# Grouped-query attention on one core: V in 8 KB rows, 64x64 PV tiles, K of two pairs' tiles with alternating heads, a loop of six steps

## The chip, the core and the metric

The kernel runs on one core of one Trainium2 chip. A core has a matrix engine (TensorE, "PE" in the profile, its weight loads "PEld"), a vector engine (VectorE, "DVE"), a scalar engine (ScalarE, "ACT"), a general engine (GpSimd, "POOL") and a sync engine (SyncE, "SP") that here only issues transfers. 16 DMA engines move data between HBM and SBUF, the on-chip memory of 128 partitions; PE writes its results to PSUM, eight banks of 512 fp32 values per partition. The metric is the time of one execution in microseconds (us), the median of several runs.

## What is computed

```python
B, Hq, Hkv, Sq, Sk, D = 16, 32, 8, 16, 2048, 128
...
k = jnp.repeat(k, rep, axis=1)
v = jnp.repeat(v, rep, axis=1)
scale = D ** -0.5
scores = jnp.einsum("bhqd,bhkd->bhqk", q, k) * scale
p = _softmax(scores, axis=-1)
return jnp.einsum("bhqk,bhkd->bhqd", p, v)
```

All tensors are bf16. Four query heads share one K/V head (`rep` is 4), so each K/V head meets 4 x 16 = 64 query rows. There are 128 K/V heads, each with 512 KB of K and 512 KB of V: 134 MB that are read once, and 4 MB of queries and outputs.

## The kernel before

**Work is done by pairs.** A pair is two neighbouring K/V heads: `NP` is 64 pairs, and the 64 query rows of both heads fill the 128 partitions. K of a pair is one transfer of 1 MB (L186), 128 rows of 8 KB: partition `a` holds 32 consecutive keys of one head, head 0 in partitions 0 to 63, head 1 in the rest. V of a pair is one transfer of 1 MB (L194) of 256 rows of 4 KB: each partition takes 16 consecutive keys of both heads. The last pair's V comes in two halves (L199). Q comes in 16 transfers of 128 KB, four pairs each, in rows of 1 KB (L207). The output of a pair is stored in rows of 256 B (L212). All these transfers are issued by SP, in one written order: in turn `t`, K of pair `t`, a Q chunk where one is due, V of pair `t - 5`, the store of pair `t - 12`. A K transfer waits until the transposed use of its buffer six pairs before is done (`sem_kt`), a V transfer until PV of eight pairs before is done (`sem_pv`), a store until the scaling of its pair is done (`sem_nm`).

**K is transposed on DVE** (L342) in 32x32 blocks, as fp32 words that each hold two bf16 values, in two instructions of 1024 words per partition. So 32 partitions of the result hold 32 pairs of head dimensions for a quarter of the keys. **Q** is copied four times side by side by POOL (L175), transposed by PE with an identity (L251) and copied out of PSUM by ACT (L380), so each group of 32 partitions has its own copy.

**Scores** (L273 and L232) take 32 matmuls of 32 rows x 64 columns and 512 moving values per pair: row group `r` goes with column group `r // 2`, so four of the array's eight 32x64 tiles are in use. Half of them (L232) reuse weights that the matmul before loaded. All four PSUM banks of `S_ps` are used, once: the next pair's scores wait until DVE has read them (`sem_max`).

**Softmax.** DVE multiplies the scores by `-scale`, writes them to `Sneg` and accumulates the minimum (L360), ACT takes the exponential and the row sum (L390) and writes bf16 values in an order in which two keys form one fp32 word. PE transposes those words (L284), eight 128x128 transposes per pair in two staging banks of `ST_ps` (a third is Q's), and ACT copies them to `PT` (L400). **PV** (L301) takes 32 matmuls of 128 rows x 64 columns and 128 moving values, one for each head and each of 16 key groups. ACT scales the result by the reciprocal of the row sum (L410; the reciprocal is DVE's, L351).

**Order on PE.** In step `p`: scores of `p + 1`, PV of `p - 3`, transposes of `p`, and in two steps of four a part of the next Q. Eight steps form the body of a hardware loop; the first steps and the last are written out. ACT's order is exponential, scaling, copies; DVE's is minimum, reciprocal, transposes of the pair after next.

## Time and profile before

| | |
|---|---|
| median of 3 runs | 343.18 us (343.05 to 344.3) |
| the profiled execution's own time | 344.2 us |
| its span, first to last instruction | 342.4 us |
| mean granted clock of PE | 0.994 |
| HBM read / written | 136.31 MB / 2.10 MB |
| K: issue to landing, median | 15.9 us |
| V: issue to landing, median | 16.5 us |
| exponential (L390), mean of one | 2494 ns |
| minimum (L360), mean of one | 2256 ns |
| K transposed, half a pair (L342), mean of one | 1222 ns |

In the profile's page, the first part gives each engine's busy time, its share of the span and its number of instructions. The second cuts the span into 40 equal slices: a digit is the busy share in tenths, 9 for 90% or more. The line on packets counts the single DMA descriptors by size. A line of a timeline has the start, the duration, the engine, the source line, the operation and its operands; in brackets stands idle time of the engine just before, and what ended it. A line of the waits has who waited for whom, the sum in us, how often, and the longest. A line of the sums by stretch has its bounds, its length, each engine's busy time and number of instructions, the granted clock, the DMA share and GB/s.

### The profile page before, as it was taken

To read this page: it belongs to the slowest core of one execution; us is meant where nothing else is said; L and a number is where in the kernel's file an instruction comes from. 1 tells how busy PE (TensorE), PEld (TensorE's weight loads), DVE (VectorE), ACT (ScalarE), POOL (GpSimd) and SP (SyncE) were. 2 spreads that over 40 slices of the span, in tenths; PEclk is the share of its full clock that TensorE was granted. 3 is DMA by queue.
4 is the path that set the end of the run, shared out by engine and by line. 5 is a ranking of instruction groups with operands and counts; after the bars stand their busy time and mean duration, and the time that the engine had idled before them with its cause. 6 is when DMAs were issued, how large, how long until landed. Compare 5 with 4: busy or idle time off the path is not lost.

```text
span 342.4 us, 9887 instructions
## 1 busy us (share of the span) xinstructions
PE 279.9 (82%) x4736; PEld 162.4 (47%) x3712; DVE 295.1 (86%) x320; ACT 267.2 (78%) x353; POOL 31.8 (9%) x23
## 2 busy tenths in 40 slices
PE   0677999999999978879788788878879778798785
PEld 0133555555455644535544544535536445455454
DVE  2489999999999998898898888988988979988940
ACT  1178889999888978878788697796887778787792
POOL 3202020202010010202002020020200102000000
PEclk9999999999999999999999999999999999999997
DMA  7999999999999999999999999999999999999993
GB/s 296 421 409 415 415 408 413 416 413 418 413 415 421 413 418 416 412 419 418 412 421 412 417 417 416 418 417 417 414 419 415 418 414 416 420 419 416 414 409 107
DMA packets 38433, 138.63 MB, mean 405 GB/s; under 512 B 11536, under 2 KB 13584, under 8 KB 30224
## 3 DMA queue, kind: packets, MB, share of 16 engines
q1 hardware_dynamic: 38416, 138.43, 100.0%
q8 instruction: 8, 0.13, 0.2%
q14 instruction: 9, 0.07, 0.1%
HBM read 136.31 MB, written 2.10 MB: 404 GB/s over the span
## 4 chain that ended last, share of the span: by engine, by line
DMA 53%; DVE 20%; issue 9%; SPq 8%; PE 8%; ACT 2%; POOL 1%
DMA Vb<-in_v_dram 47%; DVE KT L342 13%; DVE Sneg L360 6%; SPq L186 6%; DMA Kn<-in_k_dram 5%; PE O_ps L301 3%; SPq L212 2%; PE S_ps L273 1%; DMA Qn<-in_q_dram 1%; PE S_ps L232 1%; ACT O L410 1%; PE S_ps L301 1%; PE ST_ps L251 1%; PE ST_ps L284 1%; POOL Q L175 1%
## 5 line engine op out<-in xcount | busy, mean ns | idle before, releaser
L342 DVE STREAM_TRANSPOSE KT<-Kn 128x1024 f32<-128x1024 f32 x128 | 151.4, 1222 | 27.8 <-DMA Kn<-in_k_dram 27.8
L390 ACT ACTIVATE P<-Sneg,nbias 128x2048 bf16<-128x2048 f32 x64 | 159.6, 2494 | 6.3 <-DVE Sneg L360 6.3
L360 DVE TENSOR_SCALAR_CACHE_REDUCE Sneg<-S_ps 128x2048 f32<-128x2048 f32 x64 | 144.4, 2256 | 7.9 <-PE S_ps L232 7.9
L273 PE MATMUL S_ps<-KT,QT 32*64 32x512 bf16 x1024 | 106.0, 395 | 8.0 <-DVE Sneg L360 6.2
L232 PE MATMUL S_ps<-KT,QT 32*64 32x512 bf16 x1024 | 105.0, 388 | 0.0
L301 PE MATMUL O_ps<-Vb,PT 128*64 128x128 bf16 x1952 | 66.2, 221 | 36.6 <-DMA Vb<-in_v_dram 36.6
L301 PEld LDWEIGHTS O_ps<-Vb,PT 128*64 128x64 bf16 x1952 | 56.5, 110 | 78.8 <-issue 43.9
L400 ACT ACTIVATE PT<-ST_ps 128x512 f32<-128x512 f32 x128 | 69.6, 595 | 20.3 <-PE ST_ps L284 20.3
L284 PE MATMUL ST_ps<-ident,P 128*128 128x128 f32 x512 | 70.8, 282 | 4.1 <-ACT P L390 3.3
L273 PEld LDWEIGHTS S_ps<-KT,QT 32*64 32x64 bf16 x1024 | 32.5, 105 | 72.8 <-issue 62.1
L284 PEld LDWEIGHTS ST_ps<-ident,P 128*128 128x128 f32 x512 | 55.5, 142 | 13.4 <-ACT P L390 9.2
L175 POOL COPY Q<-Qn 128x2048 bf16<-128x2048 bf16 x16 | 30.3, 1896 | 255.6 <-PE ST_ps L251 251.8
L410 ACT ACTIVATE O<-O_ps,rrec 128x128 bf16<-128x128 f32 x61 | 22.5, 369 | 34.1 <-PE O_ps L301 33.9
L251 PE MATMUL ST_ps<-ident,Q 128*128 128x128 f32 x128 | 20.2, 282 | 8.8 <-POOL Q L175 8.1
L380 ACT ACTIVATE QT<-ST_ps 128x512 f32<-128x512 f32 x32 | 19.3, 603 | 8.4 <-PE ST_ps L251 8.4
L251 PEld LDWEIGHTS ST_ps<-ident,Q 128*128 128x128 f32 x128 | 15.5, 145 | 9.1 <-issue 8.0
L390 ACT ACTIVATION_READ_ACCUMULATOR P<-Sneg,nbias 128x1 f32 x64 | 13.2, 207 | 0.0
L351 DVE RECIPROCAL rrec<-rowsum 128x1 f32<-128x1 f32 x64 | 10.2, 159 | 3.0 <-ACT P L390 3.0
L301 PE MATMUL S_ps<-Vb,PT 128*64 128x128 bf16 x96 | 3.9, 243 | 2.7 <-DMA Vb<-in_v_dram 1.6
L360 DVE DVE_READ_ACCUMULATOR Sneg<-S_ps 128x1 f32 x64 | 5.4, 84 | 0.0
L301 PEld LDWEIGHTS S_ps<-Vb,PT 128*64 128x64 bf16 x96 | 3.4, 125 | 3.4 <-issue 2.3
L410 ACT ACTIVATE O<-S_ps,rrec 128x128 bf16<-128x128 f32 x3 | 1.1, 370 | 3.4 <-PE S_ps L301 3.4
(8 smaller groups left out, 3.0 us busy)
## 6 DMA issues: line engine op xcount, KB each, us to landing
Kn<-in_k_dram SPq DMA_DIRECT2D x64, 1024.0 KB, 15.9
Vb<-in_v_dram SPq DMA_DIRECT2D x63, 1024.0 KB, 16.5
Qn<-in_q_dram SPq DMA_DIRECT2D x16, 128.0 KB, 15.3
out_dram<-O SPq DMA_DIRECT2D x64, 32.0 KB, 15.4
Vb<-in_v_dram SPq DMA_DIRECT2D x2, 512.0 KB, 12.4
```

The lines of the kernel that those rows point to most:

```text
L175: gp.tensor_copy(Q4[:, :, :, :, :].rearrange("p j b r x -> p (j b) r x"), src.unsqueeze(2).to_broadcast([128, 2 * QPAIRS, 4, 64]),).then_i ...
L186: sp.dma_start(Kn[s][:, :], kf[p]).then_inc(sem_k[s], 16)
L232: return pe.add_instruction(mybir.InstMatmult(name=nc.get_next_instruction_name(), engine=mybir.EngineType.PE, ins=[pe.lower_ap(rhs), pe.l ...
L251: ins = pe.transpose(dst[:, 128 * j:128 * (j + 1)], src[:, j, b, :], ident4[:, :])
L273: ins = pe.matmul(s_ap, w, x, start=(acc == 0), stop=(acc == 3))
L284: ins = pe.transpose(dst[:, 128 * t:128 * (t + 1)], P[p % 2][:, 128 * x:128 * (x + 1)], ident4[:, :])
L301: ins = pe.matmul(o_ap(p)[64 * g:64 * (g + 1), :], pt[:, j // 2, j % 2, 64 * g:64 * (g + 1)], Vb[p % NV][:, g, j, :], start=(j == 0), stop ...
L342: ins = dve.transpose(KT[p % NKT][:, :].rearrange("p (t b e a x) -> p x e t b a", t=J // 2, b=2, e=2, x=2)[:, x, :, :, :, :], Kn[p % NK][: ...
L360: dve.tensor_scalar(Sneg[p % 2][:, :].rearrange("p (t h x) -> p h t x", t=8, h=2), S_ps[:, :].rearrange("p (h t x) -> p h t x", t=8, h=2), ...
L390: act.activation(P[p % 2][:, :].bitcast(BF16).rearrange("p (n y e) -> p n y e", n=16, e=2), Sneg[p % 2][:, :].rearrange("p (n e y) -> p n ...
L400: act.activation(PT[p % NPT][:, 4 * h:4 * (h + 1), :].rearrange("p t q -> p (t q)"), stage_ap(("P", p, h)), ACT.Copy,).then_inc(sem_ev, 1)
L410: act.activation(Osb[p % NO][:, :], o_ap(p), ACT.Copy, scale=rrec[:, p:p + 1]).then_inc(sem_nm, 1)
```

## The change

Work is still done in tiles of two K/V heads, now called units (`NU` is 64), but two units form a double pair `d` (`ND` is 32) of four neighbouring heads 0 to 3.

- *K and scores.* Unit `i` of a double pair holds heads `i` and `i + 2`. Its K is one transfer of 128 rows of 8 KB whose rows alternate between the two heads (partition `2a + g`). The transfer is made by its low-level constructor, as the source has the form 64 x 2 x 4096 and the destination 128 x 1 x 4096. DVE transposes it in one instruction of 2048 words. Each group of 32 partitions now holds a quarter of the keys of both heads, so scores run on all eight 32x64 tiles, each matmul with its own weight load; successive keys of one head lie 8 bytes apart in a moving row, 4 before.
- *V and PV.* V of two neighbouring heads is one transfer of 128 rows of 8 KB: partition `64i + a` has 32 consecutive keys of one head. A PV matmul therefore covers 64 partitions and 64 columns: 128 matmuls of a 64x64 tile for a double pair, in two halves, and the four outputs lie in two PSUM banks. V's buffers are three double pairs (six units, eight before), K's are seven (six before). V of the last double pair goes to K buffers, and its last unit is split 24 to 8 of 32 key groups.
- *Exponential and transposes.* The exponentials of a double pair's two units interleave in one `P` tile, 64 words of each in turn; 16 transposes for a double pair go through two staging banks, the second of them shared with Q (three banks before). On even steps PE waits for ACT's copy of Q (`QW`) ahead of the second group of transposes.
- *Q, stores, order.* Q comes in 32 chunks of two units, 64 KB in rows of 512 B. A store covers 64 partitions x 2 heads, still rows of 256 B. PV runs four steps behind the exponential (three before), stores 13 turns behind K (12 before). PE's loop has six steps and ten rounds, and steps that the last round lacks stand in conditional blocks. The last double pair's scaling is split between ACT and DVE.

The core of the diff:

```diff
-NK = 6
-NV = 8
...
+NK = 7
+NV = 3
+NO = 6
+NQ = 4
+NQT = 3
+NP = 3
+QPAIRS = 2
+BODY = 6
+FIRST = 6
 VLAG = 5
-PVLAG = 3
-SLAG = 12
-QLEAD = 7
+PVLAG = 4
+SLAG = 13
+LASTJ = 24
...
-    kf = k.rearrange("b h s d -> (b h s d)").rearrange("(n a x) -> n a x", n=NP, a=128)
-    vf = v.rearrange("b h s d -> (b h) (s d)").rearrange("g (a x) -> a g x", a=128)
+    kf = k.rearrange("b h s d -> (b h s d)").rearrange("(n g i a x) -> n i a g x", n=ND, g=2, i=2, a=64)
+    vf = v.rearrange("b h s d -> (b h s d)").rearrange("(n a x) -> n a x", n=NU, a=128)
...
+    for u in range(steps):
+        step_at[u] = len(pe_prog)
+        pe_prog.append(("S", u + 1))
+        if u < NU:
+            act_prog.append(("exp", u))
+        d, half = divmod(u - PVLAG, 2)
+        if u >= PVLAG:
+            pe_prog.append(("PV", d, half))
+            if half and d < ND - 1:
+                act_prog += [("norm", d, i) for i in range(2)]
+        if u % 2 == 0:
+            q_part(u, u // 2 + 2)
+        if u >= 1:
+            d, k = divmod(2 * (u - 1), 4)
+            turn(d, k)
+            if u % 2 == 0:
+                pe_prog.append(("QW", u // 2 + 2))
+            turn(d, k + 1)
...
+                sp.add_instruction(mybir.InstDMACopy(
+                    name=nc.get_next_instruction_name(), engine=mybir.EngineType.SP,
+                    ins=sp.lower_ap_dma(kf[m // 2, m % 2]), outs=sp.lower_ap_dma(Kd[s][:, :].unsqueeze(1)),
+                    queue="qSPDynamicHW", mode="Copy", cce_op=ALU.bypass,
+                )).then_inc(sem_k[s], 16)
...
+                d, g = divmod(p, 2)
+                s = d % NV
+                if d == ND - 1:
+                    sp.wait_ge(sem_kt, NU - NK + 2 + g)
+                elif d >= NV and g == 0:
+                    sp.wait_ge(sem_pv, 2 * (d - NV) + 2)
+                for x, (lo, hi) in enumerate([(0, J)] if p < NU - 1 else [(0, LASTJ), (LASTJ, J)]):
+                    dst = v_ap(d, g)[:, lo:hi, :].rearrange("a j d -> a (j d)")
+                    ins = sp.dma_start(dst, vf[p][:, D * lo:D * hi])
+                    ins.then_inc(sem_v[s] if d < ND - 1 else sem_vl[g + x], 16)
...
+                    for acc in range(4):
+                        b, e = divmod(acc, 2)
+                        for z in range(8):
+                            r, g = z % 4, (z + z // 4) % 2
+                            rows = slice(32 * r, 32 * (r + 1))
+                            at = 128 * g + 64 * i
+                            ins = pe.matmul(
+                                S_ps[64 * g:64 * (g + 1), 512 * r:512 * (r + 1)],
+                                qt[rows, b, e, at:at + 64], kt[rows, b, e, g],
+                                start=(acc == 0), stop=(acc == 3),
+                            )
...
+                for j in js:
+                    for g in gs:
+                        for i in range(2):
+                            rows = slice(64 * i, 64 * (i + 1))
                             ins = pe.matmul(
-                                o_ap(p)[64 * g:64 * (g + 1), :],
-                                pt[:, j // 2, j % 2, 64 * g:64 * (g + 1)],
-                                Vb[p % NV][:, g, j, :],
+                                o_ap(d, i)[64 * g:64 * (g + 1), :],
+                                pt[rows, j // 2, j % 2, 64 * g:64 * (g + 1)],
+                                v_ap(d, g)[rows, j, :],
...
+                dve.transpose(
+                    KT[u % 2][:, :].rearrange("p (b j a) -> p j b a", b=2, j=J),
+                    Kd[u % NK][:, :].bitcast(F32).rearrange("p (j b c) -> p j b c", b=2, c=32),
+                ).then_inc(sem_kt, 1)
...
                 dve.tensor_scalar(
-                    Sneg[p % 2][:, :].rearrange("p (t h x) -> p h t x", t=8, h=2),
-                    S_ps[:, :].rearrange("p (h t x) -> p h t x", t=8, h=2), -scale, None,
-                    op0=ALU.mult, op1=ALU.min, accum_out=nbias[:, p:p + 1],
+                    Sneg[u % 2][:, :].rearrange("p (j r a) -> p r j a", j=J, r=4),
+                    S_ps[:, :].rearrange("p (r j a) -> p r j a", j=J, r=4), -scale, None,
+                    op0=ALU.mult, op1=ALU.min, accum_out=nbias[:, u:u + 1],
```

The waits of PE, which stood in its emitting function, are now a table of their own (cut to PV and the transposes):

```diff
+        if op[0] == "PT":
+            _, d, k = op
+            u = 2 * d + 1 + k // 2
+            if k % 2:
+                return []
+            return ([(sem_ev, 2 * (u - 1))] if u > 1 else [(sem_eq, 3)]) + ([(sem_exp, u + 1)] if k == 0 else [])
+        _, d, half = op
+        if half:
+            return []
+        return ([(sem_nm, 2 * d)] if d else []) + [(sem_v[d % NV], 32 * (d // NV + 1))]
```

## The prediction

> **What bounds the kernel now.** I read the page's first parts, then the DMA view of three stretches, the sums by stretch, the waits of the second half, and the timeline of one step and of the end.
>
> ```profile
> PE 279.9 (82%) x4736; PEld 162.4 (47%) x3712; DVE 295.1 (86%) x320; ACT 267.2 (78%) x353; POOL 31.8 (9%) x23
> DMA  7999999999999999999999999999999999999993
> DMA packets 38433, 138.63 MB, mean 405 GB/s; under 512 B 11536, under 2 KB 13584, under 8 KB 30224
> q1 hardware_dynamic: 38416, 138.43, 100.0%
> ```
>
> No compute engine is full; the 16 DMA engines are, from the second slice to the last but one. The time is therefore the transfers' total, plus 1.7 us before the first packet, plus a tail. The DMA view of 12 to 18 us (K alone), of 120 to 320 us (everything) and of 322 to 331 us (V and stores) prices the packets:
>
> ```profile
> DMA packets 343, 2.55 MB, mean 425 GB/s; under 512 B 32, under 2 KB 32, under 8 KB 32
> ...
> DMA packets 22723, 83.29 MB, mean 416 GB/s; under 512 B 6907, under 2 KB 7931, under 8 KB 17747
> q1 hardware_dynamic: 22717, 83.24, 102.5%
> ...
> DMA packets 1422, 3.70 MB, mean 411 GB/s; under 512 B 550, under 2 KB 550, under 8 KB 1421
> ```
>
> K's 8 KB rows alone move 425 GB/s, V's 4 KB rows with stores 411. In 200 us there are 22723 - 17747 = 4976 K rows, 38.9 tiles of 128: one pair of heads costs 5.14 us of DMA. Now the engines against that pace:
>
> ```profile
> core 0: us, PE busy (x) PEld busy (x) DVE busy (x) ACT busy (x) POOL busy (x), PEclk, DMA share, GB/s
> 120.00:320.00 200.00, 164.02 (x2864) 95.08 (x2240) 178.78 (x193) 160.22 (x211) 16.54 (x9) 1.00 1.03 416
> ```
>
> Per pair: DVE 4.60 us, PE 4.22, ACT 4.12. The nearest, DVE, has some 0.5 us to spare; the chain in order of time shows what it can do when data is there, before 110 us: its transposes start every 4.5 us (59.95, 64.48, 69.09). After that DVE and PE wait for K and V:
>
> ```profile
> PE O_ps L301 <- DMA Vb<-in_v_dram: 35.6, 39, 1.9
> DVE KT L342 <- DMA Kn<-in_k_dram: 21.2, 38, 1.5
> ```
>
> One step of PE, and the end:
>
> ```profile
> 151.02 0.39 PE L232 MATMUL S_ps<-KT,QT 32*64 32x512 bf16 x4
> ...
> 151.25 0.39 PE L273 MATMUL S_ps<-KT,QT 32*64 32x512 bf16 x4
> ...
> 153.00 1.08 PE L301 MATMUL O_ps<-Vb,PT 128*64 128x128 bf16 x32 [1.13 <-DMA Vb<-in_v_dram]
> ...
> 334.65 1.72 PE L301 MATMUL S_ps<-Vb,PT 128*64 128x128 bf16 x32 [1.61 <-DMA Vb<-in_v_dram]
> 336.30 1.97 PE L284 MATMUL ST_ps<-ident,P 128*128 128x128 f32 x8
> 338.95 1.09 PE L301 MATMUL S_ps<-Vb,PT 128*64 128x128 bf16 x32 [0.69 <-ACT PT L400]
> 340.08 0.37 ACT L410 ACTIVATE O<-S_ps,rrec 128x128 bf16<-128x128 f32 x1 [1.18 <-PE S_ps L301]
> ```
>
> Scores go in eight groups of four, one every 0.225 us; PV takes 1.08 us. The last V packet ends at 336.7; the tail of 5.7 us is the last transposes, evacuations, PV, scaling and store.
>
> **V in 8 KB rows.** 63 tiles x 256 rows of 4 KB become 63 x 128 of 8 KB: 8064 packets fewer. In the trace's packet records the medians are 309 ns (8 KB), 159 (4 KB), 84 (2 KB), 46 (1 KB), 18 (256 B, stores) and 9 (semaphore updates); the means in the full stretch are 310 and 162 for the first two. The queue's packets sum to 102.5% of the time, so neighbours overlap: 2.5% of 3200 engine-us over 22717 packets is 3.5 ns each. Two 4 KB rows thus hold an engine for 2 x 155.5 = 311 ns by medians, 317 by means, one 8 KB row 305.5 or 306.5: 5.5 to 10 ns saved per pair, 2.8 to 5.1 us over 8064 / 16. The two pure stretches put it lower: 96000 engine-ns / 311 packets = 308 against 2 x 155, 2 ns, 1.0 us. I take 4.0: the mean and the median count equally, because I don't know whether the 4 KB packets' stretched ones (164 to 172 ns in the slowest quarter) go with the small rows. Bounds 1.0 and 5.1. [...]
>
> **Q, stores, updates.** 2048 rows of 1 KB become 4096 of 512 B. Between 18 ns and 46 ns a 512 B packet lies near 27.5, 24 without overlap: 4096 x 24 - 2048 x 42.5 = 11.3 engine-us, 0.7 us. Bounds: 0 (half the price of 1 KB) to 5.4 us (no cheaper than 1 KB); the straight line through two neighbours is nearest. 16 more transfers give 256 updates of some 5.5 ns, 0.1 us. Stores keep 8192 packets of 256 B.
>
> **K, rows of two heads alternating.** Packets keep their number and size, 128 x 8 KB. No transfer of before has a 64 x 2 source. The nearest row is V's, which alternates between two heads too: its mean is 1.7% over its median, K's 0.3%. Bounds for K: 0 and 1.7%, 2.7 us (1% of 8192 x 309 / 16 is 1.6 us). I take 0, since the V term already counts half of that stretch.
>
> DMA in sum: -4.0 + 0.7 + 0.1 = -3.2 us, bounds -5.1 and +7.2 if every bad end met.
>
> **Does the cover hold?** All that follows is hidden while transfers never run dry; its cover is 0.5 us per pair on DVE, 0.9 on PE, 1.0 on ACT.
> DVE: two transposes of 1024 (2.37 us) become one of 2048: between 2.27 (their pace in the chain) and 2.44 (2 x 1.22). Its writes become contiguous; the minimum's writes fall from runs of 128 to 16 at the same 2048 elements: 2.26 us, bounded above by +0.5, where DVE would set the pace. I take no change.
> PE, scores: 32 matmuls of 512 on eight tiles instead of four. Four row tiles start within 8 ns of each other, and PV's two column tiles over the same rows start together every 56 ns, so row and column tiles do run at once. Ends: 8 x 0.225 = 1.8 us (no gain) and 4 x 0.225 = 0.9. Twice as many weight loads go out: four start within 10 ns, beside matmuls. K's step in a moving row grows from 4 to 8 bytes; if that halved the stream, 1.8 us remains with eight tiles and 3.6 without.
> PE, PV: 64 matmuls of 128 on four tiles, 16 x 56 ns = 0.9 us if all four run, 1.8 if two do. Transposes stay at eight (1.09 us). On even steps the second staging bank is shared with Q: PE waits for ACT's 0.60 us copy less one 0.55 us transpose, 0.2 to 0.4 with signals, per two pairs; ACT's transposed copies queue behind that. Ten conditional blocks per round of six steps: a branch takes 208 to 251 ns taken and 76 not, on the sequencer, which runs ahead except behind a wait. PE's likely step is 0.9 + 0.9 + 1.09 + 0.3 + 0.2 + branches 0.15 = 3.5 us; with no extra concurrency 5.3.
> ACT: the same elements, 2.49 + 0.21 for the exponential, two copies, one scaling: no change. POOL: 32 copies of half of 1.90 us, no change.
> SP: issue order is K(t), Q, V(t-5), store(t-13). V(2d), at place 2d+5, waits for the second half of PV of d-3, run in step 2d-1, about when tile 2d+1 has landed. Behind that wait stand K(2d+6), Q and stores. Four tiles, 7 MB or some 17 us, are then already issued, as long as the 16 us from issue to landing now, so nothing runs dry. The cost is 0; with that cover gone each us of delay is a us. K has 7 buffers for 6. 225 issues of at least 0.33 to 0.44 us take 100 us of SP: hidden.
>
> **Tail.** V of the last double pair goes to free K buffers, and the last piece is 256 KB. From the last two tiles back: V(61) is seen 4.9 us before the last packet plus 0.6 (V(62) ended at 334.0 and PV began at 334.65). Then PE has PV 1.0, two transpose sets 1.1, PV 1.0, and for the last pair 32 + 24 + 8 couples of 56 ns, 3.6 us: it ends 2.4 us after the last packet, not sooner. Signal 0.15, half-row scaling 0.37 and signal on two engines, store 1.95 (340.45 to 342.4): 5.0 us, or 5.9 at the 0.8 clock of the end, against 5.7. I take -0.5; ends -1.9 (PE not late) and +0.5.
>
> **Sum.** -3.2 - 0.5 = -3.7 us. The profiled span of 342.4 becomes 338.7, its own time of 344.2 (1.0 over the median) 340.5, the median 343.18 becomes 339.5.
>
> **Rivals.**
> *No net gain (341.5 to 345.2).* V's gain is at its low end, 1.0 us, against 0.8 for Q and updates: 343.18 - 0.2 - 0.5 = 342.5; with K taking over V's stretch of 2.7 us on top, 345.2. For it: the pure stretches. Against: the means. [...]
> *Slower: the K transfer.* Its 64 x 2 source may spread rows over the engines or over SBUF partitions so that engines get in each other's way. At 1.6 us per 1%, a mean K packet above 316 ns eats the whole gain, and above 319 ns the kernel is slower by 0.5%; at 10% it takes 339.5 + 15.8 = 355 us. Against: every shape in the trace ran at 309 or 159. For: none has this shape.
> *Slower: PE sets the pace.* If the 8-byte step halves the stream and tiles don't overlap more, a step is 3.6 + 1.8 + 1.09 + 0.3 + 0.35 = 7.1 us: 64 x 7.1 + 15 = 470; it decides above 5.1. Against: two failures of what the timeline shows in parts.
> *More than forecast (below 337.5).* 5.1 on V and 1.9 on the tail, 336.9.
>
> **Numbers.** Forecast (337.5 to 341.4) 0.60; more 0.08; no net gain 0.15; K transfer 0.11; PE or DVE pace 0.06. A measurement of this kernel can tell about 0.5%, 1.7 us, from no change: faster 0.68, same 0.15, slower 0.17. The range 336.5 to 345.0 leaves out the two slower cases and the end of "more".
>
> **What would show it.** About 32400 packets in place of 38433, some 16200 of them under 8 KB, DMA still 9 in every slice but the ends, over 418 GB/s in mid-span; K packets near 309 ns; the score groups eight at a time; PE's share falling below 75%, waits for K and V longer than 35.6 and 21.2 us. I am wrong if DMA slices fall below 9 in mid-span (PE, DVE or SP's waits), or if K's packets are longer.

## The result

The changed kernel takes 345.64 us (median of 14 runs, 344.63 to 346.95); the kernel before took 342.77 us beside it on the same chip (14 runs, 342.6 to 344.3). The ratio is 1.0081, with a 95% interval of 1.0065 to 1.0097: 0.8% slower. The forecast was 339.5 us, range 336.5 to 345.0. The profiled execution has a span of 342.9 us and a time of its own of 344.64. The 14 runs lie in two groups, five from 344.6 to 345.0 us and nine from 345.5 to 347.0, and the profiled one is in the lower.

The page of the changed kernel, the lines that answer to those shown of before:

```profile
PE 285.5 (83%) x6784; PEld 162.6 (47%) x6784; DVE 294.1 (86%) x258; ACT 266.0 (78%) x353; POOL 34.3 (10%) x38
...
DMA  7999999999999999999999999999999999999991
...
DMA packets 32420, 138.66 MB, mean 404 GB/s; under 512 B 11792, under 2 KB 15888, under 8 KB 16144
...
q1 hardware_dynamic: 32400, 138.43, 98.7%
```

The packets are as many as reckoned. The time that the queue's packets took, 98.7% of 342.9 us, is 338.4 us for each of the 16 engines; it was 100.0% of 342.4. So 4.0 us of transfer work are gone, the DMA engines are as full as before, and yet the kernel isn't faster. The last slice shows where to look: 1 tenth now, 3 before. The transfers end earlier and the kernel doesn't.

The sums by stretch (bounds, length, busy time and number of instructions of PE, PEld, DVE, ACT and POOL, PE's clock, DMA share, GB/s):

```profile
0.00:20.00 20.00, 7.49 (x92) 3.44 (x100) 12.30 (x9) 6.51 (x7) 5.14 (x10) 0.91 0.90 357
...
120.00:320.00 200.00, 175.25 (x4256) 98.47 (x4263) 183.82 (x160) 165.06 (x222) 19.01 (x19) 1.00 1.02 420
320.00:332.00 12.00, 8.27 (x264) 5.13 (x248) 6.98 (x8) 10.15 (x13) 0.00 (x0) 1.00 1.02 414
332.00:345.00 13.00, 7.71 (x272) 7.01 (x272) 0.83 (x3) 3.98 (x10) 0.00 (x0) 1.00 0.21 63
```

Mid-span rose from 416 to 420 GB/s; over the same 200 us the bytes of the DMA view rose from 83.29 to 83.99 MB, 0.84%, which over the whole transfer is 2.8 us. The first packet goes out at 2.18 us instead of 1.74, since the 64 x 2 issue of the first K transfer takes SP 0.68 us instead of 0.38. The last input packet lands at 335.0 instead of 336.7: 1.7 us of the 2.8 arrive there. Behind that packet stood 5.7 us before; now it is 7.8 us.

Not all of the 5.7 us belongs to the kernel's structure. In the profile shown of before, PE's clock is halved for 3.4 us from 334.9 us on, in the middle of its end:

```profile
332.00:345.00 13.00, 5.75 (x104) 4.88 (x104) 0.16 (x1) 4.08 (x8) 0.00 (x0) 0.76 0.37 126
```

PV and eight transposes took 1.72 and 1.97 us there, where 1.08 and 1.09 are usual. Where the clock stayed up, the same structure needs 4.2 us behind the last input, as in the first two experiments below. In the changed kernel the clock stayed up (1.00), so at the same clock the end grew from 4.2 to 7.8 us.

The end of the changed kernel in order of time (start, duration, engine, line; in brackets the idle time before and what ended it):

```profile
320.13 2.31 DVE L378 STREAM_TRANSPOSE KT<-Kd 128x2048 f32<-128x2048 f32 x1 [1.07 <-DMA Kd<-in_k_dram]
...
322.36 2.25 DVE L393 TENSOR_SCALAR_CACHE_REDUCE Sneg<-S_ps 128x2048 f32<-128x2048 f32 x1
...
324.78 2.00 PE L308 MATMUL S_ps<-KT,QT 32*64 32x512 bf16 x32 [1.21 <-DVE Sneg L393]
...
326.84 2.29 DVE L393 TENSOR_SCALAR_CACHE_REDUCE Sneg<-S_ps 128x2048 f32<-128x2048 f32 x1 [2.13 <-PE S_ps L308]
...
329.39 2.45 ACT L431 ACTIVATE P<-Sneg,nbias 128x2048 bf16<-128x2048 f32 x1
...
332.08 1.07 PE L319 MATMUL ST_ps<-ident,P 128*128 128x128 f32 x8 [2.24 <-ACT P L431]
...
333.07 1.09 PE L276 MATMUL O_ps<-Vd,PT 64*64 64x128 bf16 x64
...
334.11 1.09 PE L319 MATMUL ST_ps<-ident,P 128*128 128x128 f32 x8
...
335.12 1.09 PE L276 MATMUL O_ps<-Vd,PT 64*64 64x128 bf16 x64
...
336.39 3.58 PE L276 MATMUL S_ps<-Kd,PT 64*64 64x128 bf16 x128 [0.18 <-issue]
...
340.01 0.36 ACT L460 ACTIVATE O<-S_ps,rrec 64x128 bf16<-64x128 f32 x1 [1.19 <-PE S_ps L276]
```

This is one chain from the last K tile, which lands at 320.1: its transpose, the minimum of unit 62, the scores of unit 63, their minimum, the exponential, which is done at 331.9. PE has stood 2.24 us for it. Only then come, in PE's written order, transposes, the two halves of PV of double pair 30, transposes between them, and 3.6 us of PV for double pair 31. No step of this chain waits for V: by the semaphore records V for PV of double pair 30 was there at 330.3, and that PV starts at 333.07. Before, the end did wait for V: there PE stood for the V packet of pair 62 (1.61 us, shown of before).

### The profile page after: what moved, and what is told of

The parts are those of the page before. It is cut to its first block, busy times and chain, and to the rows that moved or that the text cites. A ratio compares the mean times of both kernels' runs of the same rounds, so it can differ in the third digit from the quotient of the medians.

```text
span 342.9 us, 15390 instructions
## 1 busy us (share of the span) xinstructions
PE 285.5 (83%) x6784; PEld 162.6 (47%) x6784; DVE 294.1 (86%) x258; ACT 266.0 (78%) x353; POOL 34.3 (10%) x38
## 3 DMA queue, kind: packets, MB, share of 16 engines
q1 hardware_dynamic: 32400, 138.43, 98.7%
## 4 chain that ended last, share of the span: by engine, by line
PE 31%; DMA 23%; SPq 13%; ACT 11%; DVE 10%; issue 10%; ACTq 0%
PE S_ps L308 13%; DMA Kd<-in_k_dram 12%; DMA Vd<-in_v_dram 11%; ACT P L431 8%; PE ST_ps L319 7%; PE O_ps L276 6%; DVE KT L378 6%; SPq L251 5%; DVE Sneg L393 4%; SPq L217 3%; PE ST_ps L295 3%; SPq L241 3%; ACT QT L419 3%; SPq L232 2%; PE S_ps L276 1%
## 5 line engine op out<-in xcount | busy, mean ns | idle before, releaser
L378 DVE STREAM_TRANSPOSE KT<-Kd 128x2048 f32<-128x2048 f32 x64 | 147.3, 2302 | 18.1 <-DMA Kd<-in_k_dram 18.1
L308 PE MATMUL S_ps<-KT,QT 32*64 32x512 bf16 x2048 | 128.3, 623 | 10.6 <-DVE Sneg L393 5.9
L319 PE MATMUL ST_ps<-ident,P 128*128 128x128 f32 x512 | 75.4, 283 | 21.2 <-ACT P L431 11.9
L276 PEld LDWEIGHTS O_ps<-Vd,PT 64*64 64x64 bf16 x3968 | 58.1, 107 | 68.5 <-issue 68.5
L440 ACT ACTIVATE PT<-ST_ps 128x512 f32<-128x512 f32 x128 | 72.7, 595 | 23.1 <-PE ST_ps L319 23.0
L276 PE MATMUL O_ps<-Vd,PT 64*64 64x128 bf16 x3968 | 68.2, 218 | 15.0 <-DMA Vd<-in_v_dram 8.1
L206 POOL COPY Q<-Qn 128x1024 bf16<-128x1024 bf16 x32 | 33.4, 1042 | 265.4 <-PE ST_ps L295 136.5
L450 ACT ACTIVATE O<-O_ps,rrec 128x128 bf16<-128x128 f32 x62 | 19.2, 363 | 3.0 <-PE O_ps L276 3.0
L276 PE MATMUL S_ps<-Kd,PT 64*64 64x128 bf16 x128 | 3.6, 217 | 0.2 <-issue 0.2
L276 PEld LDWEIGHTS S_ps<-Kd,PT 64*64 64x64 bf16 x128 | 3.4, 107 | 0.3 <-issue 0.3
```

The lines of the kernel that those rows point to most:

```text
L206: gp.tensor_copy(Q4[:, :, :, :, :].rearrange("p j b r x -> p (j b) r x"), src.unsqueeze(2).to_broadcast([128, 2 * QPAIRS, 4, 64]),).then_i ...
L276: ins = pe.matmul(o_ap(d, i)[64 * g:64 * (g + 1), :], pt[rows, j // 2, j % 2, 64 * g:64 * (g + 1)], v_ap(d, g)[rows, j, :], start=(j == 0) ...
L308: ins = pe.matmul(S_ps[64 * g:64 * (g + 1), 512 * r:512 * (r + 1)], qt[rows, b, e, at:at + 64], kt[rows, b, e, g], start=(acc == 0), stop= ...
L319: ins = pe.transpose(dst[:, 128 * t:128 * (t + 1)], P[d % NP][:, 128 * y:128 * (y + 1)], ident[:, :])
L378: dve.transpose(KT[u % 2][:, :].rearrange("p (b j a) -> p j b a", b=2, j=J), Kd[u % NK][:, :].bitcast(F32).rearrange("p (j b c) -> p j b c ...
L440: act.activation(PT[d % NP][:, 4 * k:4 * (k + 1), :].rearrange("p t q -> p (t q)"), stage_ap(("P", d, k)), ACT.Copy,).then_inc(sem_ev, 1)
```

## Experiments

Ratios are to the kernel before, run beside each; its median was 342.7 to 342.9 us every time.

**V rows alone.** In the kernel before, V is read as 128 rows of 8 KB:

```diff
+    vflat = v.rearrange("b h s d -> (b h s d)").rearrange("(n a x) -> n a x", n=NP, a=128)
...
-                    dst = Vb[s][:, :, :, :].rearrange("a g j d -> a g (j d)")
-                    sp.dma_start(dst, vf[:, 2 * p:2 * p + 2, :]).then_inc(sem_v[s], 16)
+                    dst = Vb[s][:, :, :, :].rearrange("a g j d -> a (g j d)")
+                    sp.dma_start(dst, vflat[p]).then_inc(sem_v[s], 16)
```

> The kernel before with one edit: V of every pair but the last comes in 128 rows of 8 KB instead of 256 of 4 KB. The keys then lie in other places than PV expects, so the output is not the reference's; instructions and bytes are the same. Theory 1 (a packet has a price of its own, and the changed kernel lost its gain at the end): 8064 packets fewer save 2 to 4 us, here visible in full because the order of the end is the old one: 339 to 341 us against 342.8. Theory 2 (8 KB rows save nothing): 342.8, and the last V packet ends at 336.7 as before.

Measured: 339.64 us (339.37 to 341.17), ratio 0.992 (0.9898 to 0.9941). One line of the page, one of the sums by stretch, and in a third view the end in order of time:

```profile
DMA packets 30369, 138.63 MB, mean 411 GB/s; under 512 B 11536, under 2 KB 13584, under 8 KB 14096
```

```profile
120.00:320.00 200.00, 166.66 (x2896) 96.33 (x2260) 180.80 (x196) 162.35 (x214) 16.01 (x9) 1.00 1.02 421
```

```profile
331.35 1.08 PE L302 MATMUL S_ps<-Vb,PT 128*64 128x128 bf16 x32 [1.60 <-DMA Vb<-in_v_dram]
...
334.19 1.08 PE L302 MATMUL S_ps<-Vb,PT 128*64 128x128 bf16 x32 [0.74 <-ACT PT L401]
```

The 8064 packets fewer are worth 3.1 us by the medians, 3.3 us at the last input (333.4). Here the gain reaches the end, because PE waits for V there (1.60 us): what V gains, the kernel gains.

**K alternating alone.** In the kernel before, K's transfer gets the 64 x 2 source:

```diff
-    kf = k.rearrange("b h s d -> (b h s d)").rearrange("(n a x) -> n a x", n=NP, a=128)
+    kf = k.rearrange("b h s d -> (b h s d)").rearrange("(n g i a x) -> n i a g x", n=NP // 2, g=2, i=2, a=64)
...
-                sp.dma_start(Kn[s][:, :], kf[p]).then_inc(sem_k[s], 16)
+                sp.add_instruction(mybir.InstDMACopy(
+                    name=nc.get_next_instruction_name(), engine=mybir.EngineType.SP,
+                    ins=sp.lower_ap_dma(kf[p // 2, p % 2]), outs=sp.lower_ap_dma(Kn[s][:, :].unsqueeze(1)),
+                    queue="qSPDynamicHW", mode="Copy", cce_op=ALU.bypass,
+                )).then_inc(sem_k[s], 16)
```

> The kernel before with one edit: K of a tile comes as 64 x 2 rows that alternate between two heads 1 MB apart, by the same low-level transfer as in the changed kernel. Scores then belong to other keys and heads, so the output is not the reference's. Theory 1: the alternation costs little, 8 KB packets go from a mean of 309 to at most 313 ns in mid-span, 0 to 2 us: 342.8 to 344.8. Theory 3 (the K transfer ate the gain of V): packets of 316 ns or more, 346 us or later.

Measured: 343.68 us (343.02 to 344.55), ratio 1.0026 (1.0013 to 1.0038), 0.9 us slower. In the trace's packet records the median of an 8 KB packet is still 309 ns, and its mean 311.6, as before. The sums by stretch show what is lost (the first line is of before):

```profile
0.00:20.00 20.00, 7.97 (x62) 2.81 (x38) 9.33 (x8) 4.74 (x4) 5.25 (x9) 1.00 0.91 364
```

```profile
0.00:20.00 20.00, 7.73 (x60) 2.77 (x36) 9.09 (x8) 4.49 (x4) 5.25 (x9) 1.00 0.88 349
...
120.00:320.00 200.00, 165.24 (x2866) 95.62 (x2242) 179.64 (x196) 161.70 (x213) 17.05 (x9) 1.00 1.03 417
```

Mid-span is as fast as before (417 against 416 GB/s); the loss lies in the first 20 us, 0.88 busy against 0.91, 0.6 us, and the last input lands 0.6 us later (337.3 against 336.7). The other 0.3 us of the medians were not placed. In this run the alternating rows cost nothing in flight, only in being issued (0.64 us for the first K transfer on SP, 0.38 before), and the rival of a slow K transfer falls.

**Scores with a 4-byte step.** In the changed kernel, the keys of one head are taken as if they lay side by side in a moving row:

```diff
-                    kt = KT[i][:, :].bitcast(BF16).rearrange("p (b y g e) -> p b e g y", b=2, g=2, e=2)
+                    kt = KT[i][:, :].bitcast(BF16).rearrange("p (b g y e) -> p b e g y", b=2, g=2, e=2)
```

> The changed kernel with one edit: the moving row of a score matmul steps by 4 bytes, as before, and not by 8. It reads other keys, so the output is not the reference's. If the 8-byte step halves the stream, 32 score matmuls take about 1.0 us instead of 2.00; if two column tiles over the same rows share one stream, they stay at 2.00. The time moves by less than 1 us in both cases, as scores stand in the last chain only once or twice.

Measured: 344.97 us (343.73 to 346.25), ratio 1.0066 (1.0048 to 1.0084). From its end in order of time, and its costliest groups:

```profile
324.76 1.11 PE L308 MATMUL S_ps<-KT,QT 32*64 32x512 bf16 x32 [1.28 <-DVE Sneg L393]
```

```profile
L308 PE MATMUL S_ps<-KT,QT 32*64 32x512 bf16 x2048 | 76.3, 411 | 11.1 <-DVE Sneg L393 6.9 <-issue 3.3 <-ACT QT L419 0.8
```

32 matmuls take 1.11 us instead of 2.00. So the eight tiles do run at once, and the 8-byte step takes back all of what they gain: on four tiles with a step of 4 bytes the 32 matmuls took 2.0 us before (149.87 to 151.86 in its timeline). In the whole kernel 52 us of PE's time (76.3 against 128.3) are worth 0.7 us by the medians, with intervals that overlap: one link of the last chain is 0.9 us shorter.

**The last PV on four tiles.** In the changed kernel, PV of double pair 31 takes both units together:

```diff
-            for g, js in ((0, range(J)), (1, range(LASTJ)), (1, range(LASTJ, J))):
-                pe.wait_ge(sem_vl[g + (js[0] > 0)], 16)
-                pv(d, js, (g,))
+            pe.wait_ge(sem_vl[0], 16)
+            for js in (range(LASTJ), range(LASTJ, J)):
+                pe.wait_ge(sem_vl[1 + (js[0] > 0)], 16)
+                pv(d, js)
...
-                dve.wait_ge(sem_pv, 2 * d + 1 + 2 * g)
+                dve.wait_ge(sem_pv, 2 * d + 2)
```

(ACT's wait is changed like DVE's.)

> The changed kernel with one edit: the last double pair's 128 PV matmuls go out over all four tiles (both heads of a key group together) instead of one column half at a time; the scaling waits for both halves. Theory 1 (the last PV work on PE sets the end): they take 2.2 us instead of 3.58, and the time falls by 1.2 to 1.4 us against the changed kernel's 345.6. If the last V packets set the end instead, it stays at 345.6.

Measured: 345.58 us (343.92 to 346.55), ratio 1.0068 (1.0043 to 1.0093): no difference from the changed kernel that this run can tell. The end of its profiled execution:

```profile
332.29 1.85 PE L319 MATMUL ST_ps<-ident,P 128*128 128x128 f32 x8 [2.24 <-ACT P L432]
334.07 1.90 PE L276 MATMUL O_ps<-Vd,PT 64*64 64x128 bf16 x64
...
338.29 1.98 PE L276 MATMUL S_ps<-Kd,PT 64*64 64x128 bf16 x128 [0.28 <-issue]
340.37 0.75 ACT L461 ACTIVATE O<-S_ps,rrec 64x128 bf16<-64x128 f32 x2 [1.69 <-issue]
```

The last PV is 1.6 us shorter (1.98 for 3.58), but 1.1 us of that are given back behind it. Both halves of the rows are now scaled after PE has ended, one behind the other (0.75 us, 0.36 in the changed kernel, which scales the first half while PE works on the second), and so the last two stores are issued one behind the other: the last one goes out 1.54 us after PE's end, 0.47 in the changed kernel. From the start of the last PV to the end of the kernel it is 5.9 us instead of 6.5. Besides, in this execution the transposes and PV ahead of it take 1.85 and 1.90 us instead of 1.07 and 1.09: the granted clock is halved for 3.4 us from 332.4 on, behind the 2.24 us wait for the exponential. That costs 1.6 us: the next set of transposes starts 3.61 us after these, 2.03 in the changed kernel. The runs of this kernel lie in two groups like those of the changed one (here 343.9 to 344.6 and 345.6 to 346.6), which fits some executions paying this and others not. The changed kernel's profile has the same wait of 2.24 us, and its clock stays at 1.00 behind it; that the wait lowers the clock is not shown.

**PE kept busy ahead of the last transposes.** The last round of the changed kernel's loop is written out, and 16 idle transposes stand ahead of the wait for the last exponential:

```diff
+    rounds -= 1
...
+            for op in pe_prog[loop_to:]:
+                if real(op):
+                    if op == ("PT", ND - 1, 0):
+                        pe.wait_ge(sem_max, NU)
+                        for x in range(16):
+                            pe.transpose(S_ps[:, 1536:1664], ident[:, :], ident[:, :])
```

> The changed kernel with its last round written out (so without conditional blocks) and one addition: 16 idle 128x128 transposes into a free PSUM bank while PE waits for the last exponential. They add PE work of 1.8 us inside a wait of 2.2 us and feed nothing. Theory 1 (in the runs above 345 us PE's clock is halved behind that wait): the runs gather at 344.3 to 344.9 and none lies above 345.5; the median falls by 0.8 to 1.3 us from 345.6. Rival (the spread comes from elsewhere, the early clock drops or the transfers): it stays at 344.6 to 346.9. If the conditional blocks cost anything, all runs fall below 344.6.

Measured: 349.2 us (348.12 to 350.27), ratio 1.017 (1.0145 to 1.0194).

**The order of the end.** The last round is written out too, PV of double pair 30 goes to free score banks ahead of the last transposes, the last PV takes four tiles, with one scaling each on ACT and DVE:

```diff
+    rounds -= 1
...
+            ends = [op for op in pe_prog[loop_to:] if real(op)]
+            ahead = [op for op in ends if op[:2] == ("PV", ND - 2)]
+            ends = [op for op in ends if op not in ahead]
+            x = ends.index(("PT", ND - 1, 0))
+            ends[x:x] = ahead
...
```

> The changed kernel with another end: the last round is written out, PV of the last double pair but one goes ahead of the last transposes (into the score banks that are free by then), the last PV runs on all four tiles, and ACT and DVE scale one output each. Same work, same transfers. Theory 1 (behind the last exponential PE works 7.9 us in a row, of which 2.2 can go before it and 1.4 vanish): 2.2 to 3.5 us less than 345.6, 342.1 to 343.4. Rival (the last V packets, seen at 335.6, set the end): less than 1 us.

Measured: 350.0 us (348.67 to 350.28), ratio 1.0196 (1.0172 to 1.022). Both runs missed their expectation by several us, and both show the same thing. The end of the second, in order of time, and a line of its page:

```profile
321.23 0.69 PE L281 MATMUL O_ps<-Vd,PT 64*64 64x128 bf16 x34
...
323.35 0.64 PE L281 MATMUL O_ps<-Vd,PT 64*64 64x128 bf16 x30 [1.42 <-issue]
...
326.93 0.98 PE L281 MATMUL O_ps<-Vd,PT 64*64 64x128 bf16 x56
...
330.78 0.31 PE L281 MATMUL O_ps<-Vd,PT 64*64 64x128 bf16 x8 [2.87 <-issue]
```

```profile
q8 instruction: 13, 0.21, 0.3%
```

PV breaks off in the middle of its 64 matmuls, with no wait for another engine or a transfer in the trace, for 1.42 and 2.87 us (1.35 and 2.79 in the run before, at the same places). The instruction queue has 13 transfers of 16 KB instead of the changed kernel's 9; five of them come behind 318 us (at 320.9, 328.4, 333.9, 337.3 and 342.5 in the packet records), where the changed kernel has one, at 337.6. The gaps are put down to this by the author's reading: the written-out round is new code, and its transfers stand beside a full data queue (DMA slices of 9 up to 332 us in the second run). No run separates the two, and no trace shows PE waiting for these transfers. The last exponential begins at 333.1 instead of 329.4. So the runs say nothing on the order that they were to try, nor on keeping PE busy: in the first of them the clock is halved from 329.9 to 336.7 us, from within the gap of 2.79 us on, and the idle transposes start only at 334.7.

**Contiguous scores in earnest.** The kernel of the run before, with DVE writing the transposed keys of each head side by side, and the scores reading them so:

```diff
-                    kt = KT[i][:, :].bitcast(BF16).rearrange("p (b y g e) -> p b e g y", b=2, g=2, e=2)
+                    kt = KT[i][:, :].bitcast(BF16).rearrange("p (b g y e) -> p b e g y", b=2, g=2, e=2)
...
-                    KT[u % 2][:, :].rearrange("p (b j a) -> p j b a", b=2, j=J),
-                    Kd[u % NK][:, :].bitcast(F32).rearrange("p (j b c) -> p j b c", b=2, c=32),
+                    KT[u % 2][:, :].rearrange("p (b g j y) -> p j b y g", b=2, g=2, j=J),
+                    Kd[u % NK][:, :].bitcast(F32).rearrange("p (j b y g) -> p j b y g", b=2, y=16, g=2),
```

> The kernel of the end order with one edit more: DVE writes the transposed K so that the keys of one head lie 4 bytes apart, in full agreement with the scores' reading, so scores take 1.1 us instead of 2.0. The transpose's writes are scattered over two halves: between 2.30 us (no cost) and, if scattered writes cost double, 4.6. If they cost nothing, the scores of the last tile save 0.9 us of the end: 0.7 to 1.0 below the end order alone. If the transpose grows beyond 2.9 us, DVE sets the pace and the kernel takes 360 us or more.

Measured: 407.29 us (404.94 to 409.79), ratio 1.1856 (1.1822 to 1.1891). Its costliest group:

```profile
L394 DVE STREAM_TRANSPOSE KT<-Kd 128x2048 f32<-128x2048 f32 x64 | 247.0, 3860 | 5.9 <-DMA Kd<-in_k_dram 5.9
```

The transpose takes 3.86 us instead of 2.30, and DVE, 94% busy, sets a step of 6.0 us. The 8-byte step of the scores is thus the price of contiguous writes of the transpose, and here the cheaper side.

**K two turns ahead of its place.** In the changed kernel `VLAG` is 7 instead of 5, so that each K tile is issued two turns earlier against V:

> The changed kernel with one constant: V is issued 7 turns behind K and not 5, so the last K tile lands two V tiles, 4.9 us, earlier. Theory 1 (the end is set by the chain that starts with the last K tile, 22.7 us): the end comes 3 to 4.9 us earlier until the last V packet binds, 340.5 to 342.7. Rival (the last V packet or PE's work as such sets the end): within 1 us of 345.6. A third outcome: PE now waits for V in every step and V's buffers come free too late, transfers run dry in mid-span, and the time rises above 347.

Measured: 350.25 us (348.32 to 350.85), ratio 1.0212 (1.019 to 1.0234). From its waits behind 110 us (who waited, total, times, longest), where DVE no longer waits for K at all, and from its end:

```profile
PE O_ps L276 <- DMA Vd<-in_v_dram: 11.0, 13, 0.9
```

```profile
328.45 2.00 PE L308 MATMUL S_ps<-KT,QT 32*64 32x512 bf16 x32 [0.47 <-DVE Sneg L393]
...
335.75 1.06 PE L319 MATMUL ST_ps<-ident,P 128*128 128x128 f32 x8 [2.24 <-ACT P L431]
```

With K early, the scores of unit 63 come at 328.45 instead of 324.78, later. PE takes scores and PV in one order, and with no K to wait for it still waits for V every two or four steps up to 311.9 us (11.0 us in all, 8.1 in the changed kernel), so V's arrival paces the scores as well. The theory that the end is simply a chain from the landing of the last K tile falls: it runs from the last step that K or V has paced, whichever is later. What does hold is the part behind the last exponential: it begins at 333.07 instead of 329.39, and in both profiles the kernel ends 13.5 us after that.

**A short last exponential.** In the changed kernel:

```diff
+                    if u == NU - 1:
+                        dst, src = dst[:, :4], src[:, :4]
```

> The changed kernel, with the last of the 64 exponentials cut to a quarter of its columns (0.65 us instead of 2.45); the rest of that unit's weights is left as it was in the buffer, so the output isn't the reference's. Theory A, PE's order at the end: PE stands 2.2 us before the last transposes and with them PV of the last double pair but one, for nothing but this exponential. Then PE's wait falls to about 0.4 us, everything behind it moves forward by 1.8 us, the clock has less of a pause to be lowered in, and the median is 1.8 to 2.5 us below the changed kernel's 345.6: 343.1 to 343.8. Theory B, the last V packet sets the end (it lands at 335.0, and the last 128 PV start at 336.4): no more than 0.3 us comes of it, 345.3.

Measured: 343.25 us (342.94 to 344.05), ratio 1.001 (0.9994 to 1.0027), 2.4 us less than the changed kernel. Its end in order of time:

```profile
330.66 1.06 PE L319 MATMUL ST_ps<-ident,P 128*128 128x128 f32 x8 [0.62 <-ACT P L433]
...
335.01 3.58 PE L276 MATMUL S_ps<-Kd,PT 64*64 64x128 bf16 x128 [0.18 <-issue]
```

PE's wait falls from 2.24 to 0.62 us, and all that follows comes 1.4 us earlier, although V's last packet still lands at 335.2. This is theory A: the exponential sets the end, not V. The other 1.0 us of the medians fits the upper group of runs having gone (all ten lie within 1.1 us); no trace shows an upper run of the changed kernel itself, so that share is only argued.

**PV three steps behind.** In the changed kernel `PVLAG` is 3 instead of 4:

> The changed kernel with PV three steps behind the exponential instead of four, so that the first half of PV of the last double pair but one stands ahead of PE's wait for the last exponential. Nothing else is moved and the loop keeps its length. Theory A: that half (1.05 us) goes into the 2.2 us in which PE stood, and the last 128 PV start 1.0 us earlier: 344.6, less still where the clock stays up. Theory B: each step now waits for V one turn earlier, as in the run with K two turns ahead of its place, and exponentials near the end come later by up to a turn of 2.5 us: 346 to 348.

Measured: 349.01 us (347.92 to 349.8), ratio 1.0191 (1.0174 to 1.0208). From its waits behind 100 us, and its end:

```profile
PE O_ps L276 <- DMA Vd<-in_v_dram: 16.7, 13, 1.4
```

```profile
328.48 1.99 PE L308 MATMUL S_ps<-KT,QT 32*64 32x512 bf16 x32 [0.47 <-DVE Sneg L393]
...
335.78 1.06 PE L319 MATMUL ST_ps<-ident,P 128*128 128x128 f32 x8 [2.23 <-ACT P L431]
```

Theory B: V paces the scores as with K two turns ahead, and the scores of unit 63 stand at the same place, 328.48. The last exponential begins 3.7 us later than in the changed kernel, and what PV gains behind it is less: the kernel ends 13.0 us after that instead of 13.5.

**Three steps and a short tail.** The last PV on four tiles, `PVLAG` 3, and the last exponential in two halves (the row sums of the two are added by DVE):

```diff
+                    for lo, hi in [(0, 16)] if u < NU - 1 else [(0, 8), (8, 16)]:
+                        x = u + (lo > 0)
+                        act.activation(
+                            dst[:, lo:hi], src[:, lo:hi], ACT.Exp,
+                            bias=nbias[:, u:u + 1], scale=-1.0, accum_out=rowsum[:, x:x + 1],
+                        ).then_inc(sem_exp, 1)
...
```

> The changed kernel with three changes to its end and none to its transfers: PV three steps behind the exponential, the last exponential in two halves of the keys (1.35 us each) so that the first two sets of transposes can start after the first half, and the last 128 PV on all four tiles (2.0 us instead of 3.6). Theory A, the gain of the transfers was given back at the end: PE's last 128 PV start near 335.0 instead of 336.4 and take 2.0 us, so the end comes 2.6 to 3.0 us earlier: 342.6 to 343.0, the time of the kernel before or a little under. If the clock is never lowered at the end, 341.8. Theory B, V one turn earlier slows the steps: 345 or more.

Measured: 346.15 us (346.01 to 347.19), ratio 1.0098 (1.0081 to 1.0115). It is 2.9 us below the run before it by the medians of four runs each. In the profiles the stretch from the start of the last exponential to the end is 11.4 us instead of 13.0, so the shorter end is worth 1.6 us there, less than the 2.6 to 3.0 reckoned, and V's pacing takes more than that.

**Both ends.** The same with `PVLAG` 4, and the first V transfer issued ahead of the first K transfer:

```diff
+            load_v(0)
             for t in range(NU + SLAG + 1):
                 if t < NU:
                     load_k(t)
...
-                if 0 <= t - VLAG < NU:
+                if 0 < t - VLAG < NU:
```

> The changed kernel, PV four steps behind as it is, with the last exponential in two halves of the keys, the last 128 PV on four tiles, and the first V transfer, whose rows need no 64 x 2 source, issued ahead of the first K transfer. Theory A, the two ends alone hold what the transfers gained: the first packet comes at 1.75 us instead of 2.18 and the last input 0.4 us earlier; PE's last transposes begin 1.0 us after the last exponential does and not after 2.5, the last 128 PV start some 1.1 to 1.5 us earlier and take 2.0 us instead of 3.6. In sum 2.5 to 3.5 us off 345.6: 342.1 to 343.1, level with the kernel before or 0.2% under it. Theory B, V or its steps set the end as in the run with PV three steps behind: 345 or more.

Measured: 344.02 us (343.74 to 346.02), ratio 1.0033 (1.002 to 1.0046): 1.6 us better than the changed kernel, 0.9 us above the upper end of what was expected. Most of its gains weren't there. Its end:

```profile
331.04 1.36 ACT L438 ACTIVATE P<-Sneg,nbias 128x1024 bf16<-128x1024 f32 x1
...
332.64 1.06 PE L320 MATMUL ST_ps<-ident,P 128*128 128x128 f32 x8 [1.11 <-ACT P L438]
...
334.61 1.09 PE L277 MATMUL O_ps<-Vd,PT 64*64 64x128 bf16 x64 [0.91 <-ACT O L457]
```

The transposes do start 1.6 us after the exponential begins, not 2.7. But PV behind them then waits 0.91 us for ACT's scaling of the double pair before, which stands behind the second half of the exponential: it starts 3.57 us after the exponential's begin, 3.68 in the changed kernel. A wait has taken the place of the one removed. The last PV is 1.6 us shorter, but most of that is given back behind it, as in the run that changed it alone. From the start of the last exponential to the end it is 13.2 us instead of 13.5. The first packet goes out at 1.75 us, and 369 GB/s instead of 357 move in the first 20 us; yet the last input lands at 335.1, where it landed before, as mid-span moved less (83.86 against 83.99 MB between 120 and 320 us).

So this profile doesn't show where the 1.6 us of the medians come from. It has the halved clock too, from 326.9 to 330.3 us, behind a wait of 1.28 us and the 2.0 us of scores that follow it, and its own time of 346.0 is the longest of the twelve; ten of them lie below 344.3. These ten are 0.7 us below the lower group of the changed kernel (344.0 against 344.7 in the middle). The rest is that only two of twelve lie higher, and not nine of fourteen; no run shows why.

Of all that ran, V's rows alone are the fastest, but they hand PV other keys than it expects; no kernel that does the whole work beat the kernel before.

## Why the prediction was wrong

Against the profiled executions the miss is 344.64 - 340.5 = 4.1 us: 1.5 in the transfers (the last input came 1.7 us earlier, not 3.2), 2.6 in the tail (7.8 us, not 5.2). The other 2.0 us of 345.64 - 339.5 lie between profile and median: the profile of before was 1.0 us over its median, the one of the changed kernel is 1.0 under.

- **V in 8 KB rows**: right, with -4.0 taken and -3.1 to -3.3 measured by itself; the bounds of 1.0 and 5.1 held it.
- **Q, stores, updates**: right as far as the packets show, with 0.8 taken; no run measured it by itself. A 512 B packet takes 27.1 ns in the packet records, 27.5 reckoned. With 46.4 for 1 KB that is 15.9 us of engine time more, 1.0 us without overlap, 0.5 with it.
- **K alternating at 0**: right for the packets, wrong for the issue. The prediction took the issue's length on SP as hidden, which it isn't ahead of the first packet; the step costs 0.4 us there, 0.6 at the last input by itself. With -3.3, +0.6 and +0.5 the last input should have moved by 2.2 us; it moved by 1.7. The 0.5 us left were not placed.
- **Cover**: it held; the DMA slices stay at 9. Its sizes were mixed. The transpose's 2.30 us, the minimum's 2.28 and PV's 1.09 for 0.9 lie near where they were put. The scores, taken at 0.9, took 2.00: eight tiles and the half-rate stream together, the 1.8 that was named as an end. So PE's share is 83% and not below 75%, and "waits for K and V longer" is wrong as well: over the whole span PE waits 8.1 us for V (36.6 before) and DVE 18.1 for K (27.8 before). PE's longer step takes up that time: in mid-span it is busy for 175.25 of 200 us, 164.02 before. The waits, of before and then of the changed kernel:

```profile
PE O_ps L301 <- DMA Vb<-in_v_dram: 36.6, 40, 1.9
...
DVE KT L342 <- DMA Kn<-in_k_dram: 27.8, 41, 5.7
```

```profile
DVE KT L378 <- DMA Kd<-in_k_dram: 18.1, 28, 6.0
...
PE ST_ps L319 <- ACT P L431: 11.9, 30, 2.2
PE O_ps L276 <- DMA Vd<-in_v_dram: 8.1, 10, 0.9
```

- **Tail, the step that failed.** "V(61) is seen 4.9 us before the last packet ... Then PE has PV 1.0, two transpose sets 1.1, PV 1.0, and for the last pair ... 3.6." The durations are right to 0.2 us in sum; the starting point isn't. PE doesn't begin with PV when V(61) is there: the transposes that wait for the last exponential stand ahead of PV of double pair 30 in PE's order, and that exponential ends at 331.9. So that PV starts at 333.07, 2.8 us after V(61) was there (330.3). The tail was worked back from V, as it had ended in the kernel before; no chain was worked forward from the last K tile through two minimums, scores and exponential, 12 us in which DVE, PE and ACT take turns. It gives 7.8 us behind the last input, not 5.2.
- **The tail of before, misread.** The 5.7 us that the term was taken from are those of an execution with the halved clock; at full clock they are 4.2. The prediction's own 5.0 us at full clock were thus 0.8 more than before, and not 0.5 less. At the same clock the end grew by 3.6 us while the last input came 1.7 us earlier: 1.9 us slower, which is what lies between the lower group of the changed kernel (344.67 in the middle) and the kernel before (342.77). The other 1.0 us up to 345.64 goes with the upper group.
- **The other side of that error.** A deeper pipeline (four steps instead of three) and double pairs instead of pairs put more work behind the last exponential: 1.1 + 1.1 + 1.1 + 1.1 + 3.6 us on PE, where before one set of transposes and two PVs of 1.1 us were left, the first of them waiting for V anyway. In mid-span this costs nothing (420 GB/s against 416); the end pays once. That the double pair's 3.6 us weigh on the end is part of this, but four tiles for them brought only 0.5 us, because scaling and stores then stood behind. None of the rivals was this. "No net gain" had the loss in the transfers, and PE's rival had it in every step.

The cause is shown for the wait on the last exponential: shortened by 1.6 us, it gives back 1.4 us in the trace and 2.4 by the medians, and where it begins 3.7 us later (K two turns ahead), the end comes 3.7 us later. It isn't shown for the last 128 PV on half the tiles. For the halved clock it is shown that it occurs, and that it costs 1.6 us in the last PV on four tiles and 1.5 in the kernel before (5.7 us behind the last input against 4.2); that it makes the upper groups is argued. The profiles bear it out in part. Of those that lie among the longer runs of their kernel, the kernel before, the last PV on four tiles and both ends have it ahead of PE's last work; three steps and a short tail hasn't, and its last input is 0.9 us late instead. The order of the end has it in its shortest run.

## What to carry to other kernels

Where a transfer bound is relaxed, work out the end twice: back from the last transfer, and forward from the last input of the longest compute chain, through every engine's written order; the later one counts. Here the deeper pipeline and the doubled unit were free while transfers were full (420 GB/s in mid-span, 416 before) and were paid once at the end, with 3.6 us where the last input came 1.7 us earlier. Before a tail is taken from a profile, its granted clock at the end should be looked at: in the profile of before it was 0.76 behind 332 us, and 1.5 of the tail's 5.7 us went with it. PE takes K's and V's work in a fixed order here, and moving K two turns ahead let V set the pace: PE's waits for V behind 110 us rose from 8.1 to 11.0 us.

## What the runs showed that was not expected

- In the score matmuls, a moving operand read with a step of 8 bytes between bf16 values streamed at about half the rate of one with 4: 2.00 against 1.11 us for 32 matmuls of 512 on eight tiles.
- With a loop's last round written out behind it, four more pieces of 16 KB went over the instruction queue, beside the full data queue, and PE stood 1.35 to 2.87 us in the middle of a run of matmuls.
- PE's clock was halved for 3.4 us behind waits of 2.24 us (the last PV on four tiles), 1.61 us (the kernel before) and 1.28 us (both ends, with 2.0 us of scores between), and stayed at 1.00 behind the changed kernel's 2.24 us. Where it was halved, eight transposes took 1.85 us instead of 1.07.
- DVE's transpose of 2048 words took 3.86 us with scattered writes, 2.30 with contiguous ones.
- A 64 x 2 source made the first issue 0.68 us long instead of 0.38, and the first packet went out 0.4 us later.
- The last 128 PV took 1.6 us less on four tiles, and the end came only 0.5 us earlier, as the scaling of both halves and the last two stores then stood behind them.
